# Swapped query halves by transfers in SBUF, and a first layer's weights converted in smaller pieces

## The chip, the cores and the metric

The kernel runs on one core of one Trainium2 chip. The metric is the device time of one launch in microseconds (us). The core's engines are TensorE (PE; its weight loads are listed as PEld), VectorE (DVE), ScalarE (ACT), GpSimd (POOL) and SyncE (SP), which issues all transfers of this kernel.

## The reference

Attention over pooled queries, a dense layer with the mish activation, and a mixture of 8 experts whose gate is balanced by 8 rounds of row and column normalisation. All of it is float32.

```python
# attention: batch 2, 8 heads, 1152 positions, head size 64
q_pool = q.reshape(B, H, S // 2, 2, D).mean(axis=3)
scores = np.matmul(q_pool, k.transpose(0, 1, 3, 2)) / np.sqrt(D)
attn = np.exp(scores - scores.max(-1, keepdims=True))
attn = attn / (attn.sum(-1, keepdims=True) + 1e-09)
x = np.matmul(attn, v)              # to 1152 tokens x 512
# first layer: w_in 512 x 2048, w_out 2048 x 512
h = x @ w_in
x = (h * np.tanh(np.log1p(np.exp(h)))) @ w_out
# experts: w1 8 x 512 x 1024, w2 8 x 1024 x 512
P = balanced(np.exp(x @ w_gate - max))
out = sum(P[:, e:e+1] * (np.maximum(x @ w1[e], 0) @ w2[e]) for e in range(8))
```

The weights `w_in` and `w_out` of the first layer arrive as 64-bit floats and are turned into float32 on the chip.

## The kernel before

Every float32 operand of a matmul is split into a high part and a low part (`split_hi`, `split_lo`), and a product is the sum of matmuls of these parts. The program order of each engine is written out by hand.

**Attention.** Heads go in 8 pairs. The pooled queries of a pair are 9 tiles of 128 rows (tile `MID` = 4 holds rows of both heads). One tile is one tick `g`; `t` is its place in the pair, 0 to 8. In a tick TensorE computes the scores of tile g (`psS`, 6 matmuls, 12 for tile 4) into the only `ps_s` buffer, VectorE copies them out with the row minimum of the negated scores (`sc`), ScalarE takes the exponential (`e`), GpSimd normalises. Three ticks later the tile is transposed (`psT`, 9 transposes, four PSUM buffers shared with the other transposes), ScalarE copies the high part out (`eth`), VectorE the low part (`etl`), and the matmuls with v follow (`psA`; nine a tick, none in tick 7).

The scores need q as high and low part above each other along the partitions, and a second time with the two halves swapped: k stands as (high, low), and the four products of parts come from two matmuls. For that `qst` holds (high, low, high), and `trans_q` transposes each tile twice, from slices 0:2 and 1:3, two tiles to a group; ScalarE copies a group to `qT`, and tile 4 also into `qz`. The tables `PREP` (which splitting step GpSimd does at which t) and `TURN` (at which t the groups of k and q are transposed) set the places.

**Weights of the first layer.** `load_w` plans for each 128-row chunk: its transfer, two scalings on ScalarE, on VectorE a shift and a sign step, on GpSimd a join, then the high part on ScalarE and the low part on GpSimd or VectorE. `queue` holds these by engine and due tick; `run` issues those that are due. `w_in`'s first block of four chunks is converted from tick 30 on, one each 9 ticks; the first block of `w_out` at the end of attention. `T0` = 73 is the tick of the first layer's first bank.

**First layer and experts.** `mish_step` issues one bank of the first product per step, followed by output banks (`out_bank`) as far as `todo` says that they are ready. After that the gate and the experts run (line 1001 and 891 are their matmuls).

Of the kernel before, what the change touches and what calls it, by code (L numbers as in the profile page):

```python
# [23 lines left out]
def pool_attention_mish_sinkhorn_kernel(  # L24
# [12 lines left out]
    nc = tc.nc  # L37
# [76 lines left out]
        for x in ("pool", "act", "dve", "dma"):  # L114
            run(t, x)

    def load_w(which, i, times, stage, late="pool"):

        src = w_sources(i)[which].rearrange("(c p) f -> p c f", p=P)
        nm = ("wu", "wd")[which]  # L120

        def dest():
            if i not in (w1t, w2t)[which]:
                pool = wpools[f"d{0 if i == NG1 else i % 2}" if which else i % 2]
                (w1t, w2t)[which][i] = tuple(
                    pool.tile([P, 4, GF], F32R, tag=nm + x, name=f"{nm}{x}{i}") for x in "hl")
            return (w1t, w2t)[which][i]

        def hi(heng, c, x):
            split_hi(heng, dest()[0][:, c, :], x)  # L130

        def lo(c, x):
            split_lo(nc.vector if late == "dve" else nc.gpsimd, dest()[1][:, c, :], x, dest()[0][:, c, :])

        def plan64(u, t):
            box = {}

            def dma():
# [13 lines left out]
            def shift():  # L152
                t = box["t"] = wpools["t"].tile([P, GF], U32, tag="wt", name=f"wt{which}_{i}_{u}")
                nc.vector.tensor_scalar(
                    t, box["h"].bitcast(U32), 3, 0x7FFFFFF8, op0=ALU.logical_shift_left, op1=ALU.bitwise_and)

            def sign():
                nc.vector.scalar_tensor_tensor(  # L158
                    out=box["t"], in0=box["h"].bitcast(U32), scalar=0x80000000, in1=box["t"],
                    op0=ALU.bitwise_and, op1=ALU.bitwise_or)  # L160

            def join():
                t = box["t"].bitcast(I32)
                nc.gpsimd.tensor_tensor(out=t, in0=t, in1=box["l"].bitcast(I32), op=ALU.add)  # L164

            ts = t if isinstance(t, tuple) else [t + j * stage for j in range(5)]
            at(ts[0] - 2.4 * stage, "dma", dma)
            at(ts[0], "act", lambda: scale(1))
            at(ts[0], "act", lambda: scale(0))
            at(ts[1], "dve", shift)  # L170
            at(ts[1], "dve", sign)
            at(ts[2], "pool", join)
            at(ts[3], "act", lambda: hi(nc.scalar, u, box["t"].bitcast(F32)))
            at(ts[4], late, lambda: lo(u, box["t"].bitcast(F32)))

        def plan32(u, t):
            box = {}

            def dma():
                raw = box["raw"] = wraw.tile([P, 2 * GF], F32, tag="raw", name=f"raw{which}_{i}_{u}")  # L180
                nc.sync.dma_start(out=raw.rearrange("p (c f) -> p c f", c=2), in_=src[:, 2 * u:2 * u + 2, :])

            def both(j):
                x = box["raw"][:, j * GF:(j + 1) * GF]
                hi(nc.gpsimd, 2 * u + j, x)
                lo(2 * u + j, x)

            at(t[0] - 2.4 * stage, "dma", dma)
            for j in range(2):
                if i == NG1:  # L190
                    at(t[j], "act", lambda j=j: hi(nc.scalar, 2 * u + j, box["raw"][:, j * GF:(j + 1) * GF]))
                    at(t[j] + 1, "pool", lambda j=j: lo(2 * u + j, box["raw"][:, j * GF:(j + 1) * GF]))
                else:
                    at(t[j], "pool", lambda j=j: both(j))

        if i < NG1:
            for u, t in enumerate(times):
                plan64(u, t)
# [56 lines left out]
    def mish_step(k):  # L255
# [10 lines left out]
        run(T0 + k, "act")  # L266
        run(T0 + k, "dma")


    xh = xpool.tile([P, NDC, NT], F32R, tag="xh", name="xh")  # L270
    xl = xpool.tile([P, NDC, NT], F32R, tag="xl", name="xl")

    with ExitStack() as actx:
# [11 lines left out]
        st_p = spool("st", 1)  # L285
        kst_p = spool("kst", 2)
        kt_p = spool("kt", 3)
        qt_p = spool("qt", 5)
        z_p = spool("z", 1)
        ps_s = spool("ps_s", 1, space=PSUM)  # L290
        e_p = pool("e", 3)
# [49 lines left out]
        def split_q(p, eng, step, part=slice(0, QTL)):  # L341
# [8 lines left out]
            if step == 2:  # L350
                if part.start == 0:
                    qst[p] = st_p.tile([P, QTL, 3, D], F32R, tag="qst", name=f"qst{p}")
                for s in (0, 2):
                    split_hi(eng, qst[p][:, part, s, :], qs)
            if step == 3:
                split_lo(eng, qst[p][:, part, 1, :], qs, qst[p][:, part, 0, :])
# [13 lines left out]
        def trans_q(p, u):  # L370
            n = min(2, QTL - 2 * u)
            ps = ps_t.tile([P, 2, 2, P], F32R, tag="t", name=f"psq{p}_{u}")
            t = qt_p.tile([P, 2, 2, P], F32R, tag="qT", name=f"qT{p}_{u}")
            for i in range(n):
                for s in range(2):
                    nc.tensor.transpose(
                        ps[:, i, s, :], qst[p][:, 2 * u + i, s:s + 2, :].rearrange("p a d -> p (a d)"), identr)
            nc.scalar.activation(t[:, 0:n], ps[:, 0:n].bitcast(F32), AF.Copy)
            if 2 * u <= MID < 2 * u + n:
                i = MID - 2 * u  # L380
                z = qz[p % 2]
                for j in range(2):
                    nc.scalar.activation(
                        z[:, j, :, j * D:(j + 1) * D], ps[:, i, :, j * D:(j + 1) * D].bitcast(F32), AF.Copy)
            qT[p, u] = t
# [199 lines left out]
        def turn(p, t):  # L585
            fs = []
            for j in range(2):
                pp = p + (j == 0)
                if pp < NPAIR:
                    fs += [  # L590
                        lambda pp=pp, j=j, c=c: trans_k(pp, j, c)
                        for c in range(3) if TURN[f"k{j}"][c] == t + (p == 0 and j == 1)]
            for u in range(QTL // 2 + 1):
                pp = p + (u < QAHEAD)
                if pp < NPAIR and TURN["q"][u] == t:
# [95 lines left out]
    wg = const.tile([P, NDC, E], F32, name="wg")  # L691
    nc.sync.dma_start(out=wg, in_=w_gate.rearrange("(c p) e -> p c e", p=P))
    wgs = const.tile([P, NDC, 2, E], F32R, name="wgs")
    nc.gpsimd.tensor_scalar(wgs[:, :, 0, :], wg, 1.0, 0.0, op0=ALU.mult, op1=ALU.add)
    nc.gpsimd.tensor_tensor(out=wgs[:, :, 1, :], in0=wg, in1=wgs[:, :, 0, :].bitcast(F32), op=ALU.subtract)
# [385 lines left out]
```

## Time and profile before

| | |
|---|---|
| timed runs | 1263.3, 1263.29, 1259.78 us; median 1263.29 |
| the profiled execution | 1260.27 us, its span 1258.5 us |
| attention, to the first layer's first full stretch | about 0 to 276 us |
| first layer | about 276 to 500 us |
| gate and experts | to the end |

The span is the time from the first to the last instruction on the core; the launch adds the rest. In the views, "idle before" is the time in which an engine had nothing before the instruction of that row, and the name behind the arrow is what ended it. A row with x6 merges six instructions; its start is that of the first.

### The profile page before, as it was taken

Reading aid. Unit: us, or ns where it says so; the run is one execution under the profiler, and the core shown is the slowest. Engines: PE = TensorE matmul, PEld = TensorE weight load, DVE = VectorE, ACT = ScalarE, POOL = GpSimd, SP = SyncE. Lnnn points to the kernel's source line nnn. Section 1 sums busy time; section 2 is a strip of 40 time slices with the busy share of each in tenths; the row PEclk is TensorE's granted clock in tenths of the full one; section 3 lists DMA queues with packets and bytes.
Section 4 is the critical chain, followed back from the end, with each engine's and each line's share of the span. In section 5 each row is a group of like instructions: output and inputs, shape, how many; then the busy total and the mean of one; then the engine's idle time right before and its main releaser. Section 6 shows DMA issues by size and latency. Waiting matters only on the chain.

```text
span 1258.5 us, 19762 instructions
## 1 busy us (share of the span) xinstructions
PE 1241.5 (99%) x7618; PEld 1149.4 (91%) x7618; DVE 678.5 (54%) x1433; ACT 589.4 (47%) x1304; POOL 558.9 (44%) x507
## 2 busy tenths in 40 slices
PE   8999999989999999999999999999999999999998
PEld 7999999989999999898898898898898998998997
DVE  7888888884544333663543543543543543544543
ACT  7889999886644443432332332322322322422420
POOL 7787888753444331427225225224324324324320
PEclk9999999999999999999999999999999999999999
DMA  3122222222222211011111111111111111111101
GB/s 100 53 58 74 74 74 65 77 60 78 80 89 86 83 35 33 17 51 51 51 34 51 51 34 51 51 34 48 44 44 39 49 48 35 46 55 34 37 15 76
DMA packets 39086, 68.13 MB, mean 54 GB/s; under 512 B 4048, under 2 KB 13520, under 8 KB 38992
## 3 DMA queue, kind: packets, MB, share of 16 engines
q1 hardware_dynamic: 38992, 66.87, 17.4%
q8 instruction: 60, 0.98, 0.3%
q14 instruction: 34, 0.28, 0.1%
HBM read 64.50 MB, written 2.36 MB: 53 GB/s over the span
## 4 chain that ended last, share of the span: by engine, by line
PE 93%; DVE 4%; ACT 1%; issue 1%; POOL 0%; POOLq 0%; ACTq 0%; DVEq 0%
PE po L1001 32%; PE ph L214 10%; PE po L674 8%; PE psS L398 5%; PE psA L477 5%; PE psT L452 4%; PE pya L891 4%; PE pyd L891 4%; PE pyc L891 4%; PE pyb L891 4%; PE pzc L891 2%; PE pzd L891 2%; PE pza L891 2%; PE pzb L891 2%; DVE sc L403 1%; PE pxa L891 1%
## 5 line engine op out<-in xcount | busy, mean ns | idle before, releaser
L1001 PE MATMUL po<-wdl,hhall 128*128 128x512 f32 x580 | 228.8, 395 | 0.0
L1001 PE MATMUL po<-wdh,hlall 128*128 128x512 f32 x580 | 228.5, 394 | 0.0
L1001 PE MATMUL po<-wdh,hhall 128*128 128x512 f32 x580 | 228.5, 394 | 0.0
L81 POOL TENSOR_TENSOR wul<-raw,wuh 128x512 fp32r<-128x512 f32 x64 | 81.7, 1297 | 299.6 <-ACT wuh L74 299.6
L1011 DVE SCALAR_TENSOR_TENSOR oacc<-po,Pm,oacc 128x512 f32<-128x512 f32 (+1 forms) x127 | 94.6, 745 | 206.9 <-PE po L1001 206.9
L1001 PEld LDWEIGHTS po<-wdh,hhall 128*128 128x128 f32 x580 | 109.0, 188 | 26.0
L1001 PEld LDWEIGHTS po<-wdl,hhall 128*128 128x128 f32 x580 | 109.0, 188 | 24.5
L1001 PEld LDWEIGHTS po<-wdh,hlall 128*128 128x128 f32 x580 | 109.0, 188 | 24.5
L910 ACT ACTIVATE u1a<-pya 128x288 f32<-128x288 f32 x15 | 6.2, 412 | 247.2 <-PE pya L891 247.2
L458 DVE TENSOR_TENSOR etl<-psT,eth 128x384 fp32r<-128x384 f32 (+1 forms) x240 | 112.3, 504 | 14.2 <-ACT eth L455 14.0
L423 POOL TENSOR_SCALAR e<-e,rc 128x1152 f32<-128x1152 f32 x72 | 89.0, 1236 | 50.1 <-DVE rc L422 18.8
L403 DVE TENSOR_SCALAR_CACHE_REDUCE sc<-psS 128x1152 f32<-128x1152 f32 x72 | 97.4, 1353 | 17.9 <-PE psS L398 14.3
L78 POOL TENSOR_SCALAR wdh<-raw 128x512 fp32r<-128x512 f32 x60 | 37.0, 617 | 149.9 <-issue 149.9
L455 ACT ACTIVATE eth<-psT 128x384 fp32r<-128x384 f32 (+1 forms) x240 | 93.1, 480 | 6.5 <-PE psT L452 6.3
L411 ACT ACTIVATE e<-sc,nm 128x1152 f32<-128x1152 f32 x72 | 92.2, 1280 | 1.2 <-DVE rs L417 0.7
L452 PE MATMUL psT<-ident,e 128*128 128x128 f32 x648 | 85.9, 276 | 6.4 <-DVE rc L422 3.8
L81 POOL TENSOR_TENSOR wdl<-raw,wdh 128x512 fp32r<-128x512 f32 x64 | 82.9, 1295 | 13.5 <-ACT wdh L74 8.5
L398 PE MATMUL psS<-kT,qT 128*128 128x384 f32 x384 | 80.1, 343 | 3.4 <-DVE sc L403 3.4
L477 PE MATMUL psA<-etl,vst 128*128 128x256 f32 (+1 forms) x288 | 81.0, 305 | 0.3 <-DVE xs L491 0.3
L477 PE MATMUL psA<-eth,vst 128*128 128x256 f32 (+1 forms) x288 | 80.9, 304 | 0.0
L452 PEld LDWEIGHTS psT<-ident,e 128*128 128x128 f32 x648 | 70.4, 141 | 9.7 <-POOL qst L78 3.9
L164 POOL TENSOR_TENSOR wt<-wt,raw 128x512 int32<-128x512 int32 x32 | 41.9, 1310 | 78.3 <-DVE wt L158 63.7
(332 smaller groups left out, 3314.8 us busy)
## 6 DMA issues: line engine op xcount, KB each, us to landing
raw<-in_moe_w_dram SPq DMA_DIRECT2D x64, 512.0 KB, 3.7
raw<-in_moe_w_in_dram SPq DMA_DIRECT2D x16, 512.0 KB, 3.9
raw<-in_moe_w_out_dram SPq DMA_DIRECT2D x16, 512.0 KB, 3.5
kraw<-in_k_dram SPq DMA_DIRECT2D x16, 288.0 KB, 2.7
vraw<-in_v_dram SPq DMA_DIRECT2D x16, 288.0 KB, 2.8
qraw<-in_q_dram SPq DMA_DIRECT2D x7, 576.0 KB, 4.2
out_dram<-oacc SPq DMA_DIRECT2D x8, 256.0 KB, 2.0
qraw<-in_q_dram SPq DMA_DIRECT2D x1, 320.0 KB, 4.6
```

Of the source, the lines that this page charges most:

```text
L81: eng.tensor_tensor(out=lo, in0=src, in1=hi.bitcast(F32), op=ALU.subtract)
L214: nc.tensor.matmul(ps[:, 0:TH], lhsT=a, rhs=b, start=(n == 0), stop=(n == len(ops) - 1))
L398: nc.tensor.matmul(ps[:, kb, 0:TH], lhsT=a, rhs=kt[:, kb * TH:(kb + 1) * TH], start=(n == 0), stop=(n == len(ops) - 1))
L403: nc.vector.tensor_scalar(sc, ps[:, :, 0:TH], -1.0, None, op0=ALU.mult, op1=ALU.min, accum_out=nm)
L452: nc.tensor.transpose(ps[:, i, :], e[:, c * P:(c + 1) * P], ident)
L455: nc.scalar.activation(eh[:, cs, o:o + b - a], ps[:, 0:3, a:b], AF.Copy)
L458: nc.vector.tensor_tensor(out=el[:, cs, o:o + b - a], in0=ps[:, 0:3, a:b], in1=eh[:, cs, o:o + b - a].bitcast(F32), op=ALU.subtract)
L477: nc.tensor.matmul(box["ps"][:, 0:n], lhsT=vst[p, j][:, c].rearrange("p a d -> p (a d)"), rhs=(el, eh)[which][:, c, 0:n], start=(c == 0 an ...
L674: nc.tensor.matmul(ps[:, 0:TH], lhsT=a, rhs=b, start=(n == 0), stop=(n == len(ops) - 1))
L891: nc.tensor.matmul(box[bank], lhsT=a_, rhs=b_, start=bool(first and m == 0), stop=bool(last and m == len(ops) - 1), skip_group_check=True)
L1001: nc.tensor.matmul(ps[:, 0:w], lhsT=a, rhs=b[:, c, cs], start=(n == 0), stop=(n == len(ops) - 1))
L1011: nc.vector.scalar_tensor_tensor(out=oa, in0=ps[:, 0:w], scalar=gate, in1=oa, op0=ALU.mult, op1=ALU.add)
```

## The change

From pair 1 on, a q tile is transposed once, four tiles to a group. ScalarE copies the group into half 0 of `qT`, and two transfers on SP's queue copy partitions 64 to 127 of it to partitions 0 to 63 of half 1, and 0 to 63 to 64 to 127. `qz` is treated likewise. Pair 0 keeps the old way (`trans_q0`). `PREP` and `TURN` move: the q steps go to t = 1, 2, 3, 5 and the groups to t = 6 of the pair before, 1 and 2.

The shift and the sign step of the first block of `w_in` and of two chunks of `w_out` are done in two halves, each half in a tick of its own, from tick 16 on; the other two chunks of that block of `w_out` are converted in the first layer's steps. The output sums of the second quarter wait until step 9. The gate's weights are loaded and split at tick 9.

```diff
@@ load_w @@
-            at(ts[0], "act", lambda: scale(0))
-            at(ts[1], "dve", shift)
-            at(ts[1], "dve", sign)
+            at(ts[0] + parts - 1, "act", lambda: scale(0))
+            for j in range(parts):
+                cs = slice(j * GF // parts, (j + 1) * GF // parts)
+                at(ts[1] + 2 * j, "dve", lambda cs=cs: shift(cs))
+                at(ts[1] + 2 * j + parts - 1, "dve", lambda cs=cs: sign(cs))
@@ split_q @@
-                for s in (0, 2):
+                for s in (0, 2) if p == 0 else (0,):
@@ new @@
+        def swap(t):
+            for a, b in ((0, D), (D, 0)):
+                nc.sync.dma_start(out=t[a:a + D, :, 1, :].bitcast(F32), in_=t[b:b + D, :, 0, :].bitcast(F32))
+        def trans_q(p, u):
+            ps = ps_t.tile([P, 4, P], F32R, tag="t", name=f"psq{p}_{u}")
+            t, _ = q_tile(p, 4 * u)
+            n = min(4, QTL - 4 * u)
+            for i in range(n):
+                nc.tensor.transpose(
+                    ps[:, i, :], qst[p][:, 4 * u + i, 0:2, :].rearrange("p a d -> p (a d)"), identr)
+            nc.scalar.activation(t[:, :, 0, :], ps[:, 0:n].bitcast(F32), AF.Copy)
+            swap(t)
+            if 4 * u == MID:
+                middle(p, ps, 1)
+                swap(qz[p % 2])
@@ places @@
-        load_w(0, 0, evenly(30, 9), 2)
-        load_w(1, 0, [(T0 - 5, T0 - 4, T0 - 3, T0, T0 + 1), (T0 - 4, T0 - 3, T0 - 2, T0, T0 + 1),
-                     (T0 - 2, T0 - 1, T0, T0 + 1, T0 + 2), (T0 - 1, T0, T0 + 1, T0 + 2, T0 + 3)], 1, "dve")
+        load_w(0, 0, [(t, t + 2, t + 7, t + 8, t + 9) for t in evenly(16, 9)], 2, parts=2)
+        load_w(1, 0, [(t, t + 2, t + 7, T0 + j, T0 + j + 1) for j, t in enumerate((52, 60))], 2, "dve", parts=2)
+        load_w(1, 0, [None, None] + [(t, t + 1, t + 2, t + 3, t + 4) for t in (T0 + 1, T0 + 3)], 1, "dve")
-            "q0": 1, "q1": 2, "q2": 5, "q3": 6, "v00": 1, "v01": 2, "v10": 4, "v11": 7,
+            "q0": 1, "q1": 2, "q2": 3, "q3": 5, "v00": 1, "v01": 2, "v10": 4, "v11": 7,
-        TURN = {"k0": (5, 6, 7), "k1": (1, 1, 3), "q": (7, 8, 2, 2, 4)}
+        TURN = {"k0": (5, 6, 7), "k1": (2, 3, 3), "k10": (0, 0, 2), "q0": (2, 2, 3), "q": (6, 1, 2)}
@@ main loop @@
+            if g == QTL:
+                load_gate()
@@ first layer @@
-            ready = max(last + 2, NB - 1 if s == NS - 1 else 0)
+            ready = max(last + 2, NB - 1 if s == NS - 1 else 9 if s == 1 else 0)
```

On VectorE, the conversion of `w_in`'s first chunk before, in tick 5 of a pair (`sc` copies the scores out, `wt` is the converted chunk, `etl` gives the transposes' buffers back):

```order
L403 TENSOR_SCALAR sc_1973,nm_1974<-psS_1966 128x1152
L154 TENSOR_SCALAR wt_0_0_1979<-raw_0_0_1668 128x512
L158 SCALAR_TENSOR_TENSOR wt_0_0_1979<-raw_0_0_1668,wt_0_0_1979 128x512
L417 TENSOR_SCALAR rs_1962<-rs_1962 128x1
L458 TENSOR_TENSOR etl_1_1990<-psT_0_1991,eth_1_1989 128x3x128
```

And now, in ticks 0 and 1 (the second halves follow in ticks 2 and 3):

```order
L446 TENSOR_SCALAR sc_1147,nm_1148<-psS_1140 128x1152
L155 TENSOR_SCALAR wt_0_0_1150<-raw_0_0_857 128x256
L460 TENSOR_SCALAR rs_1137<-rs_1137 128x1
L501 TENSOR_TENSOR etl_2_1059<-psT_0_1153,eth_2_1058 128x3x128
L465 RECIPROCAL rc_1159<-rs_1137 128x1
L501 TENSOR_TENSOR etl_2_1059<-psT_1_1162,eth_2_1058 128x3x128
L501 TENSOR_TENSOR etl_2_1059<-psT_2_1168,eth_2_1058 128x3x128
L534 TENSOR_TENSOR xs_1023<-psA_1_1126,avt_1_1183 64x320
L446 TENSOR_SCALAR sc_1196,nm_1197<-psS_1189 128x1152
L161 SCALAR_TENSOR_TENSOR wt_0_0_1150<-raw_0_0_857,wt_0_0_1150 128x256
L460 TENSOR_SCALAR rs_1187<-rs_1187 128x1
```

Between a tile's `sc` and its first `etl` there was a whole shift and a whole sign step; now there is half of one of them.

On ScalarE, ticks 6 to 8 of a pair before (`avt` ends a group of the matmuls with v, `e` is the exponential, `kT` and `qT` are the copies of transposed k and q):

```order
L489 ACTIVATE avt_0_1028<-psA_0_963 64x256
L411 ACTIVATE e_1031,rs_1032<-sc_983,nm_984 128x1152
L366 ACTIVATE kT_0_934<-psk_0_2_1048 128x384
L455 ACTIVATE eth_1_940<-psT_0_1055 128x3x64
L455 ACTIVATE eth_2_1053<-psT_0_1055 128x3x64
L455 ACTIVATE eth_1_940<-psT_1_1066 128x3x64
L455 ACTIVATE eth_2_1053<-psT_1_1066 128x3x64
L455 ACTIVATE eth_1_940<-psT_2_1074 128x3x64
L455 ACTIVATE eth_2_1053<-psT_2_1074 128x3x64
L378 ACTIVATE qT_0_1083<-psq_0_1082 128x512
L411 ACTIVATE e_1089,rs_1090<-sc_1041,nm_1042 128x1152
L378 ACTIVATE qT_1_1107<-psq_1_1106 128x512
```

And now, with a chunk under conversion (`wuh` is its high part, `raw` a scaling of the next chunk):

```order
L532 ACTIVATE avt_0_1547<-psA_0_1484 64x256
L423 ACTIVATE qT_0_1551<-psq_0_1550 128x4x128
L454 ACTIVATE e_1559,rs_1560<-sc_1505,nm_1506 128x1152
L74 ACTIVATE wuh_1562<-wt_0_0_1150 128x512
L380 ACTIVATE kT_0_1455<-psk_0_2_1579 128x384
L498 ACTIVATE eth_1_1461<-psT_0_1586 128x3x64
L498 ACTIVATE eth_2_1584<-psT_0_1586 128x3x64
L498 ACTIVATE eth_1_1461<-psT_1_1597 128x3x64
L498 ACTIVATE eth_2_1584<-psT_1_1597 128x3x64
L498 ACTIVATE eth_1_1461<-psT_2_1605 128x3x64
L498 ACTIVATE eth_2_1584<-psT_2_1605 128x3x64
L454 ACTIVATE e_1613,rs_1614<-sc_1572,nm_1573 128x1152
```

The copy of q moved from ticks 7 and 8 into tick 6, ahead of the exponential, and the chunk's high part stands behind it.

On SP, the transfers of a pair now, from the q load on (before, the two groups of swaps were not there and the same loads followed each other):

```order
L337 DMA qraw_930<-in_q_dram 128x9x128
L414 DMA qT_0_1028<-qT_0_1028 64x4x128 x2
L329 DMA vraw_0_1050<-in_v_dram 128x576
L329 DMA kraw_0_1102<-in_k_dram 128x576
L414 DMA qT_1_1205<-qT_1_1205 64x4x128 x2
L414 DMA qz_130<-qz_130 64x2x128 x2
L329 DMA vraw_1_1265<-in_v_dram 128x576
L414 DMA qT_2_1309<-qT_2_1309 64x128 x2
L140 DMA raw_0_1_1379<-in_moe_w_in_dram 128x512
```

The swaps stand between the loads of the next operands and wait for ScalarE's copy.

## Rows read from the trace of the kernel before

**Rows 1.** The page: TensorE's busy time, and its granted clock in 40 slices.

```profile
PE 1241.5 (99%) x7618; PEld 1149.4 (91%) x7618; DVE 678.5 (54%) x1433; ACT 589.4 (47%) x1304; POOL 558.9 (44%) x507
PEclk9999999999999999999999999999999999999999
```

**Rows 2.** Busy time by window: length, PE, PEld, DVE, ACT, POOL, clock, DMA share, GB/s.

```profile
67.90:100.18 32.28, 32.16 (x251) 31.63 (x250) 28.32 (x71) 29.04 (x66) 26.06 (x25) 1.00 0.20 56
133.93:167.67 33.74, 32.80 (x252) 31.69 (x251) 30.13 (x73) 30.63 (x70) 29.15 (x27) 1.00 0.24 69
259.10:276.00 16.90, 13.03 (x87) 11.09 (x86) 16.03 (x40) 14.75 (x33) 10.10 (x8) 1.00 0.21 63
276.00:345.00 69.00, 69.00 (x407) 68.67 (x405) 32.77 (x60) 43.98 (x88) 26.52 (x22) 1.00 0.26 79
```

**Rows 3.** Timeline of TensorE: first score matmuls of pairs 2, 3 and 4.

```profile
67.90 0.52 PE L398 MATMUL psS<-kT,qT 128*128 128x384 f32 x2
...
100.18 0.34 PE L398 MATMUL psS<-kT,qT 128*128 128x384 f32 x1
...
133.93 0.34 PE L398 MATMUL psS<-kT,qT 128*128 128x384 f32 x1
```

**Rows 4.** Timeline around a chunk's shift in pair 3; last, a row of the waits.

```profile
121.25 1.44 POOL L81 TENSOR_TENSOR xl<-xs,xh 128x576 fp32r<-128x576 f32 x1
...
121.72 1.25 DVE L154 TENSOR_SCALAR wt<-raw 128x512 uint32<-128x512 uint32 x1
...
123.00 1.04 DVE L158 SCALAR_TENSOR_TENSOR wt<-raw,wt 128x512 uint32<-128x512 uint32 x1
...
124.03 0.54 DVE L458 TENSOR_TENSOR etl<-psT,eth 128x384 fp32r<-128x384 f32 x1
...
124.72 1.31 PE L452 MATMUL psT<-ident,e 128*128 128x128 f32 x9 [0.88 <-DVE rc L422]
...
PE psT L452 <- DVE rc L422: 3.8, 5, 0.9
```

**Rows 5.** Timeline of TensorE: a group of q transposes and what follows.

```profile
142.20 0.45 PE L376 MATMUL psq<-identr,qst 128*128 128x128 f32 x4
142.50 1.17 PE L452 MATMUL psT<-ident,e 128*128 128x128 f32 x9
```

**Rows 6.** Timelines of TensorE, ScalarE and VectorE in ticks 7 and 8 of pair 2.

```profile
93.47 1.21 PE L398 MATMUL psS<-kT,qT 128*128 128x384 f32 x6
...
97.04 0.67 ACT L378 ACTIVATE qT<-psq 128x512 fp32r<-128x512 f32 x1
...
99.83 0.56 DVE L458 TENSOR_TENSOR etl<-psT,eth 128x384 fp32r<-128x384 f32 x1 [0.40 <-ACT eth L455]
```

**Rows 7.** Timeline at attention's end; last, VectorE's shifts and signs from 259.1 to 276.

```profile
259.64 0.42 DVE L154 TENSOR_SCALAR wt<-raw 128x512 uint32<-128x512 uint32 x1
...
263.96 1.31 PE L398 MATMUL psS<-kT,qT 128*128 128x384 f32 x6 [1.51 <-DVE sc L403]
...
270.23 1.52 DVE L154 TENSOR_SCALAR wt<-raw 128x512 uint32<-128x512 uint32 x1 [0.54 <-ACT raw L148]
...
273.06 1.07 PE L452 MATMUL psT<-ident,e 128*128 128x128 f32 x6 [1.58 <-DVE etl L458]
...
L154 DVE TENSOR_SCALAR wt<-raw 128x512 uint32<-128x512 uint32 x3 | 2.6, 859 | 0.5 <-ACT raw L148 0.5
L158 DVE SCALAR_TENSOR_TENSOR wt<-raw,wt 128x512 uint32<-128x512 uint32 x3 | 2.1, 692 | 0.1
```

**Rows 8.** DMA issues: KB each and median us to landing; last, SP's time for an issue.

```profile
qraw<-in_q_dram SPq DMA_DIRECT2D x7, 576.0 KB, 4.2
qraw<-in_q_dram SPq DMA_DIRECT2D x2, 128.0 KB, 2.5
wg<-in_moe_w_gate_dram SPq DMA_DIRECT2D x1, 16.0 KB, 3.7
...
127.49 0.38 SPq L323 DMA_DIRECT2D qraw<-in_q_dram  x1
```

More of the change, by code (lines that the diff above doesn't have):

```diff
@@ L115, in run_all, with load_w @@
             run(t, x)
-    def load_w(which, i, times, stage, late="pool"):
+    def load_w(which, i, times, stage, late="pool", parts=1):
         src = w_sources(i)[which].rearrange("(c p) f -> p c f", p=P)
@@ L150, in scale, with shift, sign @@
                     nc.scalar.activation(box["l"].bitcast(I32), box["l"].bitcast(U32), AF.Copy, scale=2.0 ** -29)
-            def shift():
-                t = box["t"] = wpools["t"].tile([P, GF], U32, tag="wt", name=f"wt{which}_{i}_{u}")
+            def shift(cs=slice(0, GF)):
+                if "t" not in box:
+                    box["t"] = wpools["t"].tile([P, GF], U32, tag="wt", name=f"wt{which}_{i}_{u}")
                 nc.vector.tensor_scalar(
-                    t, box["h"].bitcast(U32), 3, 0x7FFFFFF8, op0=ALU.logical_shift_left, op1=ALU.bitwise_and)
-            def sign():
+                    box["t"][:, cs], box["h"][:, cs].bitcast(U32), 3, 0x7FFFFFF8,
+                    op0=ALU.logical_shift_left, op1=ALU.bitwise_and)
+            def sign(cs=slice(0, GF)):
+                t = box["t"][:, cs]
                 nc.vector.scalar_tensor_tensor(
-                    out=box["t"], in0=box["h"].bitcast(U32), scalar=0x80000000, in1=box["t"],
+                    out=t, in0=box["h"][:, cs].bitcast(U32), scalar=0x80000000, in1=t,
                     op0=ALU.bitwise_and, op1=ALU.bitwise_or)
@@ L197, in load_w @@
             for u, t in enumerate(times):
-                plan64(u, t)
+                if t:
+                    plan64(u, t)
         else:
@@ L267, in mish_step, with load_gate @@
         run(T0 + k, "dma")
+    wgs = const.tile([P, NDC, 2, E], F32R, name="wgs")
+    def load_gate():
+        wg = const.tile([P, NDC, E], F32, name="wg")
+        nc.sync.dma_start(out=wg, in_=w_gate.rearrange("(c p) e -> p c e", p=P))
+        nc.gpsimd.tensor_scalar(wgs[:, :, 0, :], wg, 1.0, 0.0, op0=ALU.mult, op1=ALU.add)
+        nc.gpsimd.tensor_tensor(out=wgs[:, :, 1, :], in0=wg, in1=wgs[:, :, 0, :].bitcast(F32), op=ALU.subtract)
     xh = xpool.tile([P, NDC, NT], F32R, tag="xh", name="xh")
@@ L287, in pool_attention_mish_sinkhorn_kernel @@
         kt_p = spool("kt", 3)
-        qt_p = spool("qt", 5)
+        qt_p = spool("qt", 2)
         z_p = spool("z", 1)
@@ L368, in trans_k, with q_tile, middle, trans_q0 @@
                 ps[:, 0:3, :].bitcast(F32).rearrange("p a d -> p (a d)"), AF.Copy)
-        def trans_q(p, u):
+        def q_tile(p, t):
+            u, i = divmod(t, 4)
+            if (p, u) not in qT:
+                n = min(4, QTL - 4 * u)
+                qT[p, u] = qt_p.tile([P, n, 2, P], F32R, tag=f"qT{n}", name=f"qT{p}_{u}", bufs=2)
+            return qT[p, u], i
+        def middle(p, ps, n):
+            z = qz[p % 2]
+            for j in range(2):
+                nc.scalar.activation(
+                    z[:, j, 0:n, j * D:(j + 1) * D], ps[:, 0:n, j * D:(j + 1) * D].bitcast(F32), AF.Copy)
+        def trans_q0(u):
             n = min(2, QTL - 2 * u)
-            ps = ps_t.tile([P, 2, 2, P], F32R, tag="t", name=f"psq{p}_{u}")
-            t = qt_p.tile([P, 2, 2, P], F32R, tag="qT", name=f"qT{p}_{u}")
+            ps = ps_t.tile([P, 2, 2, P], F32R, tag="t", name=f"psq0_{u}")
             for i in range(n):
@@ L376, in trans_q @@
                     nc.tensor.transpose(
-                        ps[:, i, s, :], qst[p][:, 2 * u + i, s:s + 2, :].rearrange("p a d -> p (a d)"), identr)
-            nc.scalar.activation(t[:, 0:n], ps[:, 0:n].bitcast(F32), AF.Copy)
+                        ps[:, i, s, :], qst[0][:, 2 * u + i, s:s + 2, :].rearrange("p a d -> p (a d)"), identr)
+            t, i = q_tile(0, 2 * u)
+            nc.scalar.activation(t[:, i:i + n], ps[:, 0:n].bitcast(F32), AF.Copy)
             if 2 * u <= MID < 2 * u + n:
[L380 to L385, printed above, removed]
+                middle(0, ps[:, MID - 2 * u], 2)
+        def swap(t):
[4 more added lines that the diff above has]
+            t, _ = q_tile(p, 4 * u)
+            n = min(4, QTL - 4 * u)
+            for i in range(n):
[6 more added lines that the diff above has]
+                swap(qz[p % 2])
         psS, scS, eS = {}, {}, {}
@@ L395, in scores @@
                 else:
-                    ops = [(qT[p, t // 2][:, t % 2, s, :], kT[p, int(t > MID)]) for s in range(2)]
+                    x, i = q_tile(p, t)
+                    ops = [(x[:, i, s, :], kT[p, int(t > MID)]) for s in range(2)]
                 for n, (a, kt) in enumerate(ops):
@@ L526, in pool_attention_mish_sinkhorn_kernel @@
         PREP = {
-            "q0": 1, "q1": 2, "q2": 5, "q3": 6, "v00": 1, "v01": 2, "v10": 4, "v11": 7,
+            "q0": 1, "q1": 2, "q2": 3, "q3": 5, "v00": 1, "v01": 2, "v10": 4, "v11": 7,
             "k00": 3, "k01": 4, "k10": 6, "k11": 8,
         }
-        PREP0 = {"q0": 2, "q1": 2, "q2": 5, "q3": 6, "k00": 3, "k10": 7, "v10": 5, "v11": 7, "k01": 3, "k11": 8}
-        TURN = {"k0": (5, 6, 7), "k1": (1, 1, 3), "q": (7, 8, 2, 2, 4)}
-        QAHEAD = 2
+        PREP0 = {"q0": 2, "q1": 3, "q2": 4, "q3": 5, "k00": 3, "k10": 7, "v10": 5, "v11": 7, "k01": 3, "k11": 8}
+        TURN = {"k0": (5, 6, 7), "k1": (2, 3, 3), "k10": (0, 0, 2), "q0": (2, 2, 3), "q": (6, 1, 2)}
         def warm(n):
@@ L557, in pool_attention_mish_sinkhorn_kernel @@
         split_kv(0, 0, "k", nc.vector, 1, False)
-        trans_q(0, 0)
+        trans_q0(0)
         warm(2)
@@ L568, in pool_attention_mish_sinkhorn_kernel @@
         scores(0)
-        for u in range(1, QAHEAD):
-            trans_q(0, u)
+        trans_q0(1)
         scores(1, ps_b)
@@ L591, in turn @@
                         lambda pp=pp, j=j, c=c: trans_k(pp, j, c)
[L592 to L595, printed above, removed]
+                        for c in range(3) if TURN["k10" if p == 0 and j == 1 else f"k{j}"][c] == t]
+            for u in range(3):
+                pp = p + (u == 0)
+                if p == 0 and TURN["q0"][u] == t:
+                    fs.append(lambda u=u: trans_q0(u + 2))
+                if 0 < pp < NPAIR and TURN["q"][u] == t:
                     fs.append(lambda pp=pp, u=u: trans_q(pp, u))
@@ L689, in out_sum @@
             split_lo(nc.gpsimd if dc % 2 else nc.vector, x2["l"][:, dc, tl], o, x2["h"][:, dc, tl])
[L691 to L695, printed above, removed]
     todo = []
```

## The prediction

> **What bounds the kernel now.** [...] In the middle of attention all four engines are nearly full, so there the order within a tick (one score tile, nine per pair) matters more than the busy share.
>
> The starts of a pair's first score matmuls give the period of a pair [rows 3]: 100.18 - 67.90 = 32.28 us for pair 2, 133.93 - 100.18 = 33.75 for pair 3. Pairs 3 to 6 are those in which one chunk of the first weight matrix is converted. So a conversion costs TensorE about 1.46 us, four times 5.8 us in all. The chain of events is in [rows 4]: VectorE runs the whole shift (1.25 us) and the whole sign step (1.04 us) between a tile's maximum and the `etl` subtractions that give the transposes' PSUM banks back; the first `etl` starts only at 124.03, and the next transposes start at 124.72 after 0.88 us of nothing. The waits between engines list five such waits, 3.8 us in total [rows 4]; the rest of the 5.8 us is what the next two ticks lose.
>
> **The change part by part.**
>
> (1) Transposes of q. From pair 1 on, a q tile is transposed once, not twice: 9 fewer in each of 7 pairs, 63 in all. Four of them hold TensorE from 142.20 to 142.50, the start of the next work, so 0.075 us each [rows 5]: 63 x 0.075 = **4.7 us**. One of these groups a pair stood in tick 7, which has no attention-times-v matmuls and is bound by VectorE, so 7 x 0.3 = 2.1 us of this may be worth nothing; against that, two evacuations by ScalarE fall away in ticks 7 and 8, where VectorE waits 0.40 us for ScalarE [rows 6]. Bounds 2.5 and 5.5; I take 4.7. GpSimd loses one of its two copies into `qst` a pair; TensorE does not wait for it, and GpSimd has time left in a pair [rows 2], so nothing.
>
> (2) Conversion in pieces. A tick now gets one half shift or one half sign. Alone, a whole shift takes 0.42 us and a sign 0.69 [rows 7], so the halves are some 0.21 and 0.35 us, an estimate from these. But the shift at 121.72 took 1.25 us, and it ended 0.28 us after GpSimd's 1.44 us subtraction that ran from 121.25 [rows 4]: it was held until GpSimd was done. A half can be held as long as a whole one, so a half shift costs VectorE between 0.21 and 0.21 + 0.83 = 1.04 us. What does a tick take without loss? The old burst of 2.29 us cost 1.46, so 0.83 us was absorbed. A half of 1.04 then costs 0.2, and one of 0.21 nothing. Six chunks go through attention now (four of the first matrix, two of the second); at two shift halves each, mostly short of the worst, I take 0.3 us a chunk, and 0.1 for ScalarE, whose copy of the converted chunk now falls into tick 6 beside the evacuation of q. New cost 6 x 0.4 = 2.4, less where the two late chunks leave out that copy: 2.0. Gain 5.8 - 2.0 = **3.8 us**; bounds 5.8 and 5.8 - 6 x 1.46 = -3.0 (each chunk as dear as before).
>
> [...]
>
> (3) End of attention. The four chunks of the second matrix stood there: between 259.1 and 276 VectorE is busy 16.03 of 16.90 us, the fullest engine of that stretch [rows 2], and three shifts and three signs are in it, 2.6 and 2.1 us of busy time [rows 7]. TensorE waits 1.51 us for a maximum and 1.58 us for an `etl` right behind the shift that took 1.52 [rows 7]. Two chunks move to earlier pairs, two into the first layer. With these 4.7 us taken from the bound engine, TensorE can win no more than its idle 3.87 and some thin spots; pairs without conversions still have a tick 7 that VectorE bounds. Bounds 1.5 (that tick and the last tile's own chain stay) and 4.7; I take **3.9 us**.
>
> (4) The two chunks in the first layer, with the output sums of its second quarter made to wait until step 9. In that layer TensorE is at 69.00 of 69.00 us and VectorE at 32.8, ScalarE at 44.0, GpSimd at 26.5 [rows 2]; this is the cover. Per chunk VectorE adds 0.42 + 0.69 us plus the low part. TensorE has 12 matmuls of the next bank to do in each step meanwhile, and the four sums left out at steps 5 and 6 are done later: zero, bounds 0 and -2 us (two matmul groups waiting once for a late chunk).
>
> (5) The transfers. Each swap moves 128 KB in 512-byte runs between the halves of the partitions, two per tile group, on SP's queue. No row shows a transfer within SBUF; the nearest is the q load of the same size, 128 KB in 512-byte runs, 2.5 us to landing, and the whole q load of 576 KB takes 4.2 [rows 8]. What it must hide in: the group is transposed at the end of tick 6, so tick 7 starts 0.3 us later than the 93.47 of [rows 6], at 93.8; its evacuation (0.67 us, as `qT` there) ends near 94.7, two issues of 0.38 us [rows 8] bring 95.5, and the first use is the second score matmul of the next pair, about 100 (100.18 in [rows 3], less what ticks 7 and 8 lose). That leaves 4.3 us for a landing of 2.5 (bounds 2.5 and 4.2, and less than 2.5 changes nothing): hidden, zero, at either bound. The `qz` swaps have three ticks and are safer. Queued behind a swap on SP, which waits for ScalarE, stand only the loads of v and k of the pair after, needed several ticks later. [...]
>
> (6) The gate's weights are loaded in tick 9 of attention. GpSimd waits for them; the load lands in 3.7 us [rows 8]. GpSimd has 32.28 - 26.06 = 6.2 us free in such a pair [rows 2], and its normalised tile is needed two ticks after it is made. Zero, bounds 0 and -1.
>
> Sum: 4.7 + 3.8 + 3.9 = **12.4 us**. The profiled execution took 1260.27 us, so 1247.9 by its own time; the median of the three timed runs is 1263.29, 3.0 us above it, and from there it is 1250.9. I forecast 1250, two thirds of the way to the median; the rivals' times are taken at the same place.
>
> **The rivals.**
>
> A. Held pieces: every half shift waits out a GpSimd instruction, or ScalarE falls behind in ticks 6 to 8, and the six chunks cost as much as before. For it: the 1.25 and 1.52 us shifts, GpSimd busy 29.15 of 33.74 us in such pairs [rows 2]. Against: in a pair before its conversions GpSimd is busy only 26.06 of 32.28 us [rows 2], and the joins and low parts come five ticks later than the pieces. Term (2) is -3.0, the gain 5.6, the time 1257.
>
> B. The end of attention doesn't get shorter, since the last tiles' own chain (maximum, exponential, normalise, transpose) binds it. For it: VectorE has 16.03 - 4.7 = 11.3 us of other work there. Term (3) is 1.5, the time 1252.
>
> C. Slower: the swaps land late. If a landing takes more than 4.3 us, TensorE stands at the first tile of 7 pairs for the difference. Slower by 0.3% needs 12.4 + 3.8 = 16.2 us, 2.3 a pair, so a landing of 6.6 us. No q load takes more than 4.2 in the median [rows 8], and transfers have the engines to themselves for most of the time (DMA share 0.20 to 0.24 [rows 2]). At that point 1267.
>
> D. No change: VectorE, with 28.32 us of work in a 32.28 us pair before any conversion [rows 2], is the true bound in most ticks, the removed transposes free nothing, and the waits move from one tick to the next. Term (1) falls to 1, (2) to 0, (3) to 1.5: 1260.
>
> **How the numbers follow.** A measurement of this kernel tells 0.3% (3.8 us) from no change. Chances: my forecast 0.63, A 0.13, B 0.10, C 0.05, D 0.09. Range: own time less all upper bounds (5.5 + 5.8 + 4.7 = 16.0 us) is 1244, A is 1257; 1245 to 1257 leaves out C, D and a little of either edge. Faster by more than 0.3% (under 1259.5): the forecast, A, B, 0.86. Within: most of D, 0.08. Slower: C and an unnamed remainder, 0.06.
>
> **What the profile of the changed kernel would show.** (1) 81 transposes of q on TensorE in place of 144. (2) Pair periods of 31.5 to 32 us in pairs 2 to 6, with no wait of transposes near 0.9 us; half shifts well under 1 us. A shows as half shifts of 1 us and pairs over 33 us. (3) TensorE idle under 1 us from tick 66 to the first layer. (4) No idle TensorE in the first layer. (5) Swaps landing in 2 to 3 us, no score matmul waiting for a DMA. D would show as scores waiting for VectorE's maximum in most ticks. The prediction is wrong above all if the engines beside TensorE, all near 90% in attention, can't follow a tick that is 0.7 us a pair shorter.

## The result, and the profile after

The changed kernel takes 1249.68 us (median of 6 runs, 1249.21 to 1250.66); the kernel before, timed beside it, takes 1261.54 (6 runs, 1259.66 to 1263.3). The ratio is 0.9907 with a 95% interval of 0.9894 to 0.9919: faster by 0.9%. The span fell from 1258.5 to 1247.4 us. The forecast was 1250.0, faster.

The page of the changed kernel, TensorE's line and its clock, answers to [rows 1]: 63 matmuls fewer, the granted clock at 9 of 10 or more in all slices and 1.000 on average, as before.

```profile
PE 1235.4 (99%) x7555; PEld 1144.7 (92%) x7555; DVE 680.8 (55%) x1445; ACT 579.9 (46%) x1290; POOL 553.6 (44%) x500
PEclk9999999999999999999999999999999999999999
```

The timeline of TensorE after: the first score matmul of pairs 1, 2, 3 and 7, that of the last tile, and one of attention's last matmuls (start, length, engine, line).

```profile
35.42 0.51 PE L441 MATMUL psS<-kT,qT 128*128 128x384 f32 x2
...
67.10 0.52 PE L441 MATMUL psS<-kT,qT 128*128 128x384 f32 x2
...
99.28 0.45 PE L441 MATMUL psS<-kT,qT 128*128 128x384 f32 x1
...
228.71 0.44 PE L441 MATMUL psS<-kT,qT 128*128 128x384 f32 x1
...
256.30 0.62 PE L441 MATMUL psS<-kT,qT 128*128 128x384 f32 x2 [0.50 <-DVE sc L446]
...
265.77 0.31 PE L520 MATMUL psA<-etl,vst 128*128 128x320 f32 x1
```

The timeline of before has three starts that [rows 3, 7] don't show: those of pairs 1 and 7, and the `psA` matmul that answers to the last row above.

```profile
35.62 0.68 PE L398 MATMUL psS<-kT,qT 128*128 128x384 f32 x3
...
235.12 0.69 PE L398 MATMUL psS<-kT,qT 128*128 128x384 f32 x3
...
276.89 0.31 PE L477 MATMUL psA<-etl,vst 128*128 128x320 f32 x1
```

Differences of these starts are the budget. A pair without a conversion is pair 1: 67.10 - 35.42 = 31.68 us, before 67.90 - 35.62 = 32.28. Pair 2 converts a chunk now: 32.18. Pairs 3 to 6 take (228.71 - 99.28) / 4 = 32.36, before (235.12 - 100.18) / 4 = 33.74. In the changed kernel pairs 2 to 5 convert the four chunks of `w_in`, pair 6 and the start of pair 7 the two of `w_out`. At the last tile's scores the gain is 263.96 - 256.30 = 7.7 us, at attention's last matmul 276.89 - 265.77 = 11.1. So all of the 11.1 us of span is won in attention, 3.5 of it behind the last scores.

The waits between engines after (engine, tile, line, what it waited for; us in total, times, longest) no longer have the transposes' wait for VectorE that [rows 4] closes with.

```profile
PE psS L441 <- DVE sc L446: 4.0, 9, 1.5
...
PE po L720 <- DVE hlall L81: 0.6, 1, 0.6
```

The windows after: pair 2, the last 16.9 us of attention, the first layer (columns as in [rows 2]). TensorE's idle time at the end of attention is 0.62 us in place of 3.87, and the layer has 0.60.

```profile
67.10:99.28 32.18, 31.86 (x242) 30.82 (x240) 29.89 (x75) 29.28 (x67) 26.80 (x25) 1.00 0.38 95
248.90:265.80 16.90, 16.28 (x123) 15.69 (x122) 15.45 (x42) 13.76 (x33) 10.95 (x10) 1.00 0.10 32
265.80:335.00 69.20, 68.60 (x402) 68.25 (x402) 37.60 (x63) 45.92 (x92) 29.27 (x23) 1.00 0.27 84
```

The transfers after, by the DMA view (issues, KB, median us to landing), and SP's time for two swap issues.

```profile
qT<-qT SPq DMA_DIRECT2D x28, 128.0 KB, 2.5
qz<-qz SPq DMA_DIRECT2D x14, 64.0 KB, 2.1
...
93.63 1.29 SPq L414 DMA_DIRECT2D qT<-qT  x2
```

What a conversion still costs (32.18 us in pair 2 and 32.36 on average in pairs 3 to 6, against 31.68) stands mostly in this timeline of ScalarE and VectorE in pair 2: the copy `wuh` of the converted chunk goes first, `kT` and `eth` after it, and `etl`, which frees the transposes' banks, waits 0.80 us for `eth`.

```profile
94.74 0.62 ACT L74 ACTIVATE wuh<-wt 128x512 fp32r<-128x512 f32 x1
...
95.26 0.48 ACT L380 ACTIVATE kT<-psk 128x384 fp32r<-128x384 f32 x1
...
95.63 1.43 ACT L498 ACTIVATE eth<-psT 128x192 fp32r<-128x192 f32 x6
96.21 0.62 DVE L501 TENSOR_TENSOR etl<-psT,eth 128x192 fp32r<-128x192 f32 x2 [0.80 <-ACT eth L498]
```

Pair 6 has no such copy, and yet takes 32.43 us by its score starts. There a scaling of the next chunk stands ahead of `kT` and `eth`:

```profile
224.10 0.70 ACT L148 ACTIVATE raw<-raw 128x512 f32<-128x512 f32 x1
...
225.64 0.62 DVE L501 TENSOR_TENSOR etl<-psT,eth 128x192 fp32r<-128x192 f32 x2 [0.87 <-ACT eth L498]
```

And the second half shift of a chunk, in pair 3, is held as long as a whole one was (1.25 us [rows 4]): it takes 1.35 us and ends 0.15 us after GpSimd's subtraction.

```profile
108.69 1.44 POOL L81 TENSOR_TENSOR vst<-vraw,vst 128x576 fp32r<-128x576 f32 x1
...
108.93 1.35 DVE L155 TENSOR_SCALAR wt<-raw 128x256 uint32<-128x256 uint32 x1
```

### The profile page after: what moved, and what is told of

Read it like the earlier page. It is cut to its first block, busy times and chain, and to the rows that moved or that the text cites. A ratio compares the mean times of both kernels' runs of the same rounds, so it can differ in the third digit from the quotient of the medians.

```text
span 1247.4 us, 19732 instructions
## 1 busy us (share of the span) xinstructions
PE 1235.4 (99%) x7555; PEld 1144.7 (92%) x7555; DVE 680.8 (55%) x1445; ACT 579.9 (46%) x1290; POOL 553.6 (44%) x500
## 4 chain that ended last, share of the span: by engine, by line
PE 96%; DVE 2%; issue 1%; ACT 1%; POOL 1%; POOLq 0%; DVEq 0%; ACTq 0%
PE po L1041 32%; PE ph L220 10%; PE po L720 8%; PE psS L441 7%; PE psA L520 6%; PE psT L495 5%; PE pya L931 4%; PE pyd L931 4%; PE pyc L931 4%; PE pyb L931 4%; PE pzd L931 2%; PE pzc L931 2%; PE pza L931 2%; PE pzb L931 2%; DVE sc L446 1%; PE pxa L931 1%
```

## The experiments

The theory after the result: the gain is the three terms of the forecast, and what a conversion still costs is ScalarE's copy. The rivals: the held halves cost it, or the swaps do. Ratios are to the kernel before, timed beside each experiment.

**The transfers alone.** The kernel before, with q transposed once, the swaps, and their tables `PREP`, `PREP0` and `TURN` (in which groups of k move too); the conversions whole and where they were. The gate's weights are loaded at tick 9, as in the change. Two places of the edit:

```diff
@@ PREP @@
-            "q0": 1, "q1": 2, "q2": 5, "q3": 6,
+            "q0": 1, "q1": 2, "q2": 3, "q3": 5,
@@ trans_q @@
+            swap(t)
```

> The single transposes with the swaps and their places, but the first layer's weights converted as before (whole steps, from tick 30, w_out's first block at the end of attention). If the terms add: the span falls from 1258.5 by 4 to 5 us, to about 1254, and a pair with a conversion still takes some 33 us. If VectorE is the true bound of the ticks and the removed transposes free nothing: 1257 to 1258, with more scores waiting for VectorE's maximum.

1260.05 us, ratio 0.9993 (0.9983 to 1.0002), span 1258.3: nothing won. Pairs 1 and 2, which convert nothing here, take 31.68 us, as pair 1 does after, so the transposes pay there; in pairs 3 to 6, where a chunk is converted, it is lost again: pair 3 takes 132.68 - 98.85 = 33.83 us, no less than the 33.75 of before. Pair 5 takes 35.25, 1.4 more than its neighbours, with a lower clock (0.71 and 0.87 in two windows, last section). Two of the ten executions have a recorded granted clock of 1.0 over the whole run; their spans are 1256.4 and 1256.7 us, so 1.6 to 1.9 us are won where the clock holds. Timeline of pair 3, and the row of the waits:

```profile
98.85 0.52 PE L441 MATMUL psS<-kT,qT 128*128 128x384 f32 x2
...
121.10 1.60 POOL L81 TENSOR_TENSOR qst<-qraw,qst 128x576 fp32r<-128x576 f32 x1
121.45 1.79 DVE L161 SCALAR_TENSOR_TENSOR wt<-raw,wt 128x512 uint32<-128x512 uint32 x1
...
123.92 1.31 PE L495 MATMUL psT<-ident,e 128*128 128x128 f32 x9 [1.80 <-DVE rc L465]
...
132.68 0.51 PE L441 MATMUL psS<-kT,qT 128*128 128x384 f32 x2
...
PE psT L495 <- DVE rc L465: 7.5, 5, 1.8
```

The sign step, 0.69 us when alone [rows 7], takes 1.79: q's last low part, moved from tick 6 to tick 5, now runs on GpSimd just then. The sign step ends 0.54 us after it, and TensorE waits 1.80 us where it waited 0.88 [rows 4].

**The same with the conversion earlier.** Only the conversions' times move: they start 14 ticks earlier, in pairs 2 to 5, with the join, the copy and the low part at the changed kernel's distances; the steps stay whole.

```diff
-        load_w(0, 0, evenly(30, 9), 2)
+        load_w(0, 0, [(t, t + 2, t + 7, t + 8, t + 9) for t in evenly(16, 9)], 2)
```

> As e1_transfers_only (transposes once and swaps, whole conversions, second matrix at the end of attention), but the four conversions of the first matrix start 14 ticks earlier, with the whole shift and the whole sign in tick 1 of a pair and not in tick 6, where GpSimd now makes q's fourth low part. Theory (e1 lost the 4.5 us of the transposes because the whole shift and sign meet that low part): tick 6 of pairs 2 to 6 goes back to about 3.3 us, tick 1 grows to about 4.35 as in e3_whole_steps, no transposes wait 1.8 us for VectorE, the span is 1253 to 1254. Rival (the swaps or GpSimd's load take the gain, wherever the conversion stands): 1257 to 1259 again.

1255.65 us, ratio 0.9957 (0.9942 to 0.9972), span 1252.5, 0.5 below the range of the theory. Between the profiled runs 5.8 us come back, 1.4 of them pair 5's clock; between the ratios it is 0.36%, 4.5 us. (Tick 6 is 3.64 us, not 3.3, since the one group of q stands in it, as after; tick 1 is 4.35.) Timeline of a chunk in pair 2: shift and sign run at their own 0.42 and 0.69 us, and GpSimd, idle for 2.62 us, has nothing until 71.83.

```profile
66.70 0.68 PE L441 MATMUL psS<-kT,qT 128*128 128x384 f32 x3
...
69.89 0.42 DVE L155 TENSOR_SCALAR wt<-raw 128x512 uint32<-128x512 uint32 x1
...
70.34 0.69 DVE L161 SCALAR_TENSOR_TENSOR wt<-raw,wt 128x512 uint32<-128x512 uint32 x1
...
71.83 1.23 POOL L466 TENSOR_SCALAR e<-e,rc 128x1152 f32<-128x1152 f32 x1 [2.62 <-PE psq L421]
...
99.50 0.62 PE L441 MATMUL psS<-kT,qT 128*128 128x384 f32 x2
```

Pair 2 is 99.50 - 66.70 = 32.80 us, so whole steps in the good place cost 0.6 a chunk more than the pieces (32.18). Of the 1.1 us over a pair without a conversion, the shift and the sign make 0.7 (tick 1, 4.35 for 3.66), the copy in tick 8 the rest.

**The changed kernel with whole steps.** The two calls lose `parts=2`.

> The changed kernel with shift and sign of the six early chunks whole and in one tick; their places stay. If pieces are what removes the wait: each chunk pays up to 1.46 us again where it now pays about 0.6, so 3 to 5 us more, a span of 1251 to 1252. If a held half costs as much as a held whole, so that cutting buys nothing: within 0.5 us of 1247.4.

1254.44 us, ratio 0.9946 (0.9931 to 0.9961), span 1252.0. The pieces are worth 4.6 us of span, at the upper end of what was expected: 0.6 in each of pairs 2 to 5, and 2.0 in pairs 6 and 7 (33.53 and 28.46 us by the score starts, after 32.43 and 27.59), where the last chunk's steps fall.

**The pieces without the transfers.** The changed kernel with two transposes a tile and the tables of before.

> Two transposes of each q tile as before, but the weights converted as in the change (pieces, two chunks of w_out in the layer), and the gate's weights loaded at tick 9. If the terms add: the span is 1247.4 + 4.5, about 1252. If the whole gain is VectorE's: 1247 to 1249.

1253.83 us, ratio 0.9942 (0.9925 to 0.9958), span 1252.0: 6.5 us of the 11.1. With 0.2 us for the transfers alone, the parts do not add up: 4.4 us are won only when both are there, or some 2.7 if the transfers alone are credited with the 1.9 us of their best execution. Its waits have a new row, five times: TensorE's transposes of q's first group in tick 7 wait for ScalarE's `kT`, which stands behind the copy (in pair 6 behind a scaling):

```profile
PE psq L391 <- ACT kT L381: 3.2, 5, 0.7
```

**The q steps alone.** Of the table, only q's rows move, in the kernel before.

```diff
-            "q0": 1, "q1": 2, "q2": 5, "q3": 6,
+            "q0": 1, "q1": 2, "q2": 3, "q3": 5,
```

> The kernel before with GpSimd's steps for q alone moved to t = 1, 2, 3, 5; two transposes, no swaps, weights converted as before. If the transfers alone brought nothing because q's last step on GpSimd then stood beside the shift and the sign step and held them: the wait in tick 6 of four pairs grows from 1.2 to 2 us here too, a span of 1261 to 1263. If the swaps were to blame: 1258.5, as before.

1273.75 us, ratio 1.0104 (1.0087 to 1.0121), and not for the reason expected: all pairs from 1 to 6 are slower, those without conversions too. The first row below is of the waits, the second the window of pair 1.

```profile
PE psk L365 <- POOL kst L81: 14.0, 7, 2.3
...
35.55:71.88 36.33, 34.05 (x251) 33.12 (x250) 28.44 (x71) 29.25 (x66) 25.91 (x24) 0.95 0.18 50
```

By the code, q's step 2 at tick 3 must wait until the old `qst` has been read by the transposes of tick 4, and k's low part stands behind it on GpSimd; the trace shows only that `psk` waits for k's low part. So this run says nothing of the collision in the first experiment, whose own rows and the second experiment do.

**The second matrix at the end of attention again.** All four chunks as before, and the output sums' `ready` too.

> The changed kernel with all four chunks of w_out's first block converted at the end of attention as before, and no output sums held back. If VectorE's shifts and signs there are what TensorE waited for: some 3.9 us of waits come back, less 1.2 us that two chunks cost in earlier pairs and 0.8 us that the layer loses now: a span of 1249 to 1250. If the last tile's own chain sets the end of attention: 1246 to 1247.4, no worse than the changed kernel.

1252.37 us, ratio 0.9933 (0.9918 to 0.9948), span 1250.5, 3.1 us above the changed kernel, 0.5 above the range that was expected. Pair 6 is 0.65 us shorter without its chunk, the layer's wait for `hlall` is gone, and the two waits of [rows 7] are back, by the timeline:

```profile
256.25 1.33 PE L441 MATMUL psS<-kT,qT 128*128 128x384 f32 x6 [1.52 <-DVE sc L446]
...
265.37 1.07 PE L495 MATMUL psT<-ident,e 128*128 128x128 f32 x6 [1.60 <-DVE etl L501]
```

**The copy three ticks later.** In the changed kernel only the copy and the low part of the first matrix's chunks move.

```diff
-        load_w(0, 0, [(t, t + 2, t + 7, t + 8, t + 9) for t in evenly(16, 9)], 2, parts=2)
+        load_w(0, 0, [(t, t + 2, t + 7, t + 11, t + 12) for t in evenly(16, 9)], 2, parts=2)
```

> The changed kernel, but ScalarE's copy of each converted chunk of w_in stands in tick 0 in place of tick 6, and the low part three ticks later. If that copy, ahead of the copies out of tick 7's transposes, is what makes tick 8 of a pair with a conversion 0.43 us longer: four such ticks, 1.7 us, a span of 1245.7, with tick 8 at 3.46 us. If the pieces on VectorE cause it: no change, 1247.4.

1247.31 us, ratio 0.9891 (0.9876 to 0.9905), span 1245.3. Timeline of pair 2: `kT` comes without the copy ahead of it, `etl` waits 0.29 us, and the pair takes 98.58 - 66.84 = 31.74 us, 0.06 from a pair with no conversion. Here the copy was the remaining cost. Pairs 3 to 5 win 0.61, 0.51 and 0.65 us; 0.1 of it is tick 3, where the second half shift now meets another step of GpSimd (the low part, which moved with the copy) and takes 0.74 us in pair 3. Pair 6, with the scaling in the copy's place, still takes 32.17 us.

```profile
66.84 0.52 PE L441 MATMUL psS<-kT,qT 128*128 128x384 f32 x2
...
94.46 0.49 ACT L380 ACTIVATE kT<-psk 128x384 fp32r<-128x384 f32 x1
...
95.42 0.62 DVE L501 TENSOR_TENSOR etl<-psT,eth 128x192 fp32r<-128x192 f32 x2 [0.29 <-ACT eth L498]
...
98.58 0.52 PE L441 MATMUL psS<-kT,qT 128*128 128x384 f32 x2
```

**The second half shift three ticks after the first.** `ts[1] + 3 * j` in place of `2 * j` in the changed kernel.

> The changed kernel with the second half of each shift and sign one tick later (ticks 3 and 4). If the second half shift takes 1.3 us because GpSimd's subtraction for v runs beside it, it takes about 0.3 us here, and tick 3 loses its 0.1 us: span 1246.5 to 1247.4. If a half in any tick is held: it stays at 1 us or more.

1249.03 us (one run), span 1247.1. The half shift is free of GpSimd now (timeline of pair 3), 0.29 us in place of 1.35, and the tick gets 0.1 us back, no more: in this place a held half costs TensorE next to nothing.

```profile
112.54 0.29 DVE L155 TENSOR_SCALAR wt<-raw 128x256 uint32<-128x256 uint32 x1
```

**The first group's swap a tick later.** `"q": (7, 1, 2)` in `TURN`.

> The changed kernel with a pair's first group of q transposed, copied and swapped in tick 7, one tick later. Copied about 97.7 on the clock of the changed kernel's pair 2, issued by 98.9, landed 2.5 us later at 101.4, needed at 99.4: TensorE waits some 2 us in each of 7 pairs, a span of 1258 to 1262. If the swaps are ready much earlier than I count: 1247 to 1249.

1258.06 us (one run), span 1256.3, between the two ranges that were named and nearer to the first. TensorE now waits for the swap in each of the 7 pairs, 1.3 us and not 2, by the waits:

```profile
PE psS L441 <- DMA qT<-qT: 8.9, 7, 1.5
```

So a swap is hidden with room of less than one tick: tick 7 is 2.76 us long in the changed kernel, and moving the swap past it leaves 8.9 / 7 = 1.3 us uncovered.

**Two attempts at more.** The kernel with the later copy, and the first layer's first output sums held back a step more (`last + 2 + (s == 0)`); then that with the second half shift later as well.

> As e5_copy_later (copy and low part of a converted chunk three ticks later), and the output sums of the first layer's first quarter also wait one step more. Theory (the 0.6 to 0.8 us stand of TensorE in the layer is the output matmul that needs the low part of a late chunk, and the chunk only needs a little more time): span 1244.4 to 1244.8, 0.6 us under e5. Rival (the stand only moves to the next output matmul): 1245.3 as e5.

> As e8_copy_later_layer, and the second half shift comes three ticks after the first, not two, where GpSimd does not hold it. Theory (a held half shift costs its tick little): 0.2 to 0.4 us under e8, as e7_second_half_later was under the changed kernel. Rival (the freed VectorE time counts more once ScalarE is out of the way): 1 us under e8. Third: nothing, within 0.1 us.

Without and with the later half shift: 1247.95 us (0.9898, 0.9884 to 0.9913), span 1245.1, and 1248.8 us (0.9902, 0.9885 to 0.9918), span 1246.4. The first is its rival's case: the stand in the layer only moves, to the evacuation of a bank, by the timeline:

```profile
282.98 0.44 PE L720 MATMUL po<-hhall,wdl 128*128 128x384 f32 x1 [0.63 <-ACT acc L727]
```

The second is none of the three that were expected: ticks 5 and 6 of pairs 3 to 6 grow by 0.1 to 0.3 us. The second half sign now runs in tick 4 beside k's low part, but it did so too where only the half shift was later, and tick 5 did not grow there; the cause stays open. The later copy alone has the lowest median, 1247.31; its interval overlaps that of the changed kernel, so the 2.1 us between them rest on the spans and the pair starts, not on the timed runs.

## Why the prediction was right, and where its sizes were off

The time was right, 1249.68 for 1250.0, inside 1245 to 1257, and the three gains were seen where they were forecast. That the number fits to 0.3 us is luck in part: the forecast starts from 1262.4 us and wins 12.4, while the kernel before took 1261.54 beside the changed one and the span fell by 11.1. Three of its signs failed: pairs 2 to 6 take 32.2 to 32.4 us and not 31.5 to 32, a second half shift takes 1.35 us and not well under 1, and TensorE is idle in the layer for 0.60 us. And the terms were added as if each stood by itself, which two of the experiments refute. The terms, from the starts above:

1. **Transposes**, 4.7 forecast. Pairs 1 to 6 win 32.28 - 31.68 = 0.60 each, 3.6; what comes before pair 1 wins 0.2, and pair 7 another 0.2 beside its wait. Together 4.0: the estimate of 0.075 us each was a little high for what reaches the path. What it did not see is that the term depends on term 2: with the conversions left in place it is 0.2 in the profiled run, or up to 1.9 in the runs with a clock of 1.0. The prediction counted GpSimd's steps as busy time in a pair and did not ask which instruction of VectorE each of them meets; with `q3` at tick 5 its low part meets the sign step.
2. **Conversion in pieces**, 3.8 forecast. Before, 4 x (33.74 - 32.28) = 5.8 us; after, 0.50 + 4 x (32.36 - 31.68) = 3.2, where 2.0 was put. Gain 2.6. This is the mis-sized term, and the split behind it was the wrong way round: 0.3 us a chunk was put on the held halves and 0.1 on ScalarE's copy. The second half shift is held as feared (1.35 us) and costs 0.1; ScalarE costs the rest, 0.4 to 0.5, because the copy, or in pair 6 a scaling, stands ahead of `kT` and `eth`. The row that could have told it was there: VectorE already waited 0.40 us for ScalarE in tick 8 [rows 6]. (By its own parts the new cost was 2.4 less two copies of 0.1, which is 2.2 and not 2.0; and C's time at the common place is 1266, not 1267.)
3. **End of attention**, 3.9 forecast. The wait for a maximum at the last tile's scores falls from 1.51 to 0.50, and behind them the stretch shortens from 276.89 - 263.96 = 12.93 to 265.77 - 256.30 = 9.47 us. Gain 4.5, near the upper bound.
4. **Two chunks in the layer**, 0 forecast, bounds 0 and -2: -0.6, one wait of an output matmul for `hlall`. VectorE's sign step ahead of it is held again (1.80 us, 0.69 when alone [rows 7]), in this timeline after the change:

```profile
275.76 1.48 POOL L81 TENSOR_TENSOR xl<-xs,xh 128x576 fp32r<-128x576 f32 x1
276.00 1.80 DVE L161 SCALAR_TENSOR_TENSOR wt<-raw,wt 128x512 uint32<-128x512 uint32 x1
277.72 1.47 DVE L81 TENSOR_TENSOR hlall<-ph,hhall 128x384 fp32r<-128x384 f32 x3
...
278.32 0.44 PE L720 MATMUL po<-hhall,wdl 128*128 128x384 f32 x1 [0.60 <-DVE hlall L81]
```

5. **Swaps and gate load**, 0 forecast: no wait for either. The landing of 2.5 us was taken from the right row [rows 8]; an issue takes 1.29 / 2 = 0.6 us, not the 0.38 assumed, which the room absorbed.

The sum is 4.0 + 2.6 + 4.5 - 0.6 = 10.5; the other 0.5 us to the 11.1 of span lie in the gate and the experts. From the `pyd` matmul behind TensorE's last wait (0.9 us for ScalarE, the same in both) to the end of the span it is 702.1 us before and 701.6 after; the transfers alone have 701.8 and the copy three ticks later 702.2. What makes this difference stays open; between kernels with the same code there it is as large. The errors of terms 1, 2 and 4 (-0.7, -1.2, -0.6) were partly made up by 3 and by that.

Of the rivals, A was half right: ScalarE does fall behind, but the chunks of pairs 2 to 6 cost 3.2 us in all, where A has 1.46 each, and pairs take 32.4, not over 33 us. B is refuted by the idle 0.62 us. C had a mechanism that exists, since a tick later the swaps are waited for. D's time is what the transfers alone give, but by another way: not VectorE as a general bound, but its two instructions for a chunk, held once a pair.

## What to carry to other kernels

Before an engine's step is moved to another tick, look at which instructions of the engine that holds it stand there: here the same whole shift and sign cost 2.1 us a chunk beside GpSimd's low parts (tick 6 of pair 3 by the score starts, 5.74 for 3.64) and 0.7 where GpSimd is idle. Cutting them in that better place won 0.6 us a chunk more. And when a burst is cut up, ask of each piece not how long it lasts but which chain it stands in: a 1.35 us piece with slack behind it was nearly free, a 0.62 us copy ahead of two evacuations was most of what remained.

## What the runs showed of the hardware

A swap between the partition halves, 128 KB from 64 partitions to the other 64, lands in 2.5 us, the same as a q load of that size [rows 8]. The q load starts in another memory (`in_q_dram`), so the two medians don't single out what the way between the halves takes. Such an issue keeps SP for 0.6 us, half of the 1.29 us of two.

TensorE's granted clock has a mean of 1.000 in the profiled executions of both kernels. In two experiments it was lower for a stretch. With the transfers alone it is 1.00 from 184 to 190 us, 0.71 and 0.87 in the two windows around and behind the wait of 1.79 us in pair 5, which ends at 191.55 (below, columns as in [rows 2]), and 1.00 again from 198 to 202. From 193.85 to 194.70 the `psA` matmuls of 256 columns start 0.21 us apart, in pair 3 of that run 0.12. Pair 5 took 1.4 us longer than pairs 3, 4 and 6, whose waits stand in the same row (5 times, 7.5 us, 1.8 at most). The run with the q steps alone has a pair at 0.95 (above) and another at 1.00 (142.95 to 177.72 us), with seven waits in one row, 2.3 us at most. What decides between them isn't settled here.

```profile
190.00:194.00 4.00, 2.45 (x12) 2.43 (x13) 4.00 (x10) 1.61 (x4) 2.19 (x3) 0.71 0.50 143
194.00:198.00 4.00, 4.00 (x30) 3.75 (x28) 2.76 (x6) 2.63 (x6) 2.62 (x2) 0.87 0.06 12
```
